# A new order of the first batches, and h as 384 and 192 columns with g stored by units of 192 tokens

## The chip, the cores and the metric

The kernel runs on one NeuronCore of a Trainium2 chip. The metric is the device time of one execution in microseconds. TensorE (PE) multiplies into PSUM; its weight loads have a row of their own in the profile (PEld). VectorE is DVE, ScalarE is ACT, GpSimd is POOL, and SyncE (SP) issues all transfers.

## The reference

```python
# 8 batches, 8 heads, 576 tokens, 64 per head, 32 memory slots
a = exp(phi - max over tokens);  a = a / (sum over tokens + 1e-9)
k_m, v_m = a^T @ k, a^T @ v                       # per head: 32 x 64
attn = softmax((q @ k_m^T) / 8);  y = attn @ v_m
x = y as 4608 x 512
x = relu(x @ w_in1)**2 @ w_out1                   # 512 -> 2048 -> 512
out = silu(x @ w_in2) @ w_out2                    # 512 -> 2048 -> 512
```

All arrays are float32; the four weights come as 64-bit words, of which the kernel makes float32.

## The kernel before

The program has four stages, one after the other: attention fused with the first product (the "first stage", up to about 318 us), the second product with squares taken of g (L889), the third product (L1003), and the fourth (L889 again). The last three use a scheme of seven products for eight and run in blocks of 384 tokens (TH).

**First stage.** For each batch of 576 tokens the value part of the attention is folded into the first weights: `piece` (L546) multiplies the small `v_m` into 512 columns of `w_in1`, and ACT and DVE cut the result into a high and a low float32r half (`wp`). The softmaxed scores, turned, are the moving operand, again as high and low half (`attnT`). `first_product` (L649) makes one tile h per 128 of the 2048 columns: 112 such tiles for batches 1 to 7, numbered by t, each of twelve matmuls, six (two row groups times high-high, high-low, low-high) for each half of the tokens, and a half is 288 columns. h lies in two PSUM banks, one half in each, and there are two h buffers. One ReLU on ACT (L671) writes a row of g into `gt`, and after each second row `to_rows` (L616) sends the pair to the DRAM array `g1`, where 1.5 blocks of 384 tokens make a batch: two transfers, of 384 and of 192 tokens, with a run of 1536 or 768 bytes for each row of the pair on each partition.

Batch 0 goes another way (`first_by_halves`, L626): four tiles t share a group of 512 columns, each with two columns of 128 and one span of the tokens, 256 or 320 of them (`SPANS0`), so that work begins before all tokens have their scores. Its scores are made by token (`scores_by_token`, L502) and turned on PE (`turn_attn`, L530). Weights of batch 0 are loaded in units (`load_unit`, L264; `unit`, L278, makes float32 of one on ACT and DVE).

**Order.** Things are put into a table `sched` by `at(time, function)`, and the table is emptied in order of time between the tiles t: entries below 0 come before the first tile. `START` (L50), the list `tail` in `front` (L310), `UNITS0`, `PIECES0` (L52), `PLAN`, `PLAN1` and `PLAN2` (L54 to L62) hold the times. The tile framework then sets the final order on each engine by its own plan; `follow` adds only an order, `after` and `hold` add a real wait. `in_order` chains the loads of the start. `pe` chains the matmuls before the first tile, and `idle` (L300) puts in matmuls of no use that keep PE busy there. `join` (L451) sets where the first matmul of a front's group comes on PE.

**Buffers that matter.** `kv` has one buffer, so the loads of batch 2's kv have to wait for the product of batch 1; `h` has two, `gt` four.

Of the kernel before, what the change touches and what calls it, by code (L numbers as in the profile page):

```python
# [21 lines left out]
P = 128  # L22
# [4 lines left out]
HALF = S // 2  # L27
NF = DFF // P
NC = 5
# [5 lines left out]
TB, TH = 6, 384  # L35
NQ = NF // 2
# [8 lines left out]
CHUNKS0 = ((0, P), (2 * P, 3 * P, S - P))  # L45
SPANS0 = ((0, 2 * P), (2 * P, S))


IDLE = {2: 7, 3: 6, 4: 7}
START = ("phi", "kv", "idle15", "max", "rows", "idle3", "exp", "idle18", "product", "q", "q", "w0", "w1", "q", *(f"w{n}" for n in range(2, 8)))  # L50
UNITS0 = (6, 6, 7, 7, 9, 9, 10, 10)
PIECES0 = {0: (1, 0), 1: (1, 1), 7: (2, 0), 8: (2, 1), 10: (3, 0), 12: (3, 1)}  # L52
# [25 lines left out]
def attention_moe_moe(ctx: ExitStack, tc, q, kv, phi, w_in1, w_out1, w_in2, w_out2, out):  # L78
# [231 lines left out]
    def front(b):  # L310
# [7 lines left out]
        def load_phi():  # L318
# [3 lines left out]
            held(nc.sync.dma_start(t[:, :NC - 1], phi[b, :n].rearrange("(p c e) -> p c e", p=P, e=2 * P)))  # L322
            held(nc.sync.dma_start(t[:rows(NC - 1), NC - 1], phi[b, n:].rearrange("(p e) -> p e", e=2 * P)))

        def load_kv(c):
# [7 lines left out]
            (hold if b > 1 else in_order)(nc.sync.dma_start(t.rearrange("p k e d -> p (k e d)"), kv[b, c * P:c * P + n]))  # L333
# [11 lines left out]
        def load_q(r):  # L345
            if b == 0:
                if r == 0:
                    st["q"] = apool.tile([P, NP, S], F32, tag="at", name="q")
# [3 lines left out]
            (hold if begun else in_order)(nc.sync.dma_start(t, q[b, r]))  # L352
# [45 lines left out]
        def kv_product(*gs):  # L398
# [4 lines left out]
            for c, g in ((c, g) for c in range(NC) for g in gs):  # L403
                n = rows(c)
                for p in range(NP):
# [5 lines left out]
                    join(mm, c == g == p == 0, new=True)  # L411
# [58 lines left out]
        def scores(r):  # L470
# [12 lines left out]
            nc.scalar.activation(e, e, AF.Exp, scale=1.0 / float(D) ** 0.5)  # L483
# [8 lines left out]
        def transpose_attn(r):  # L492
# [6 lines left out]
            nc.scalar.copy(hi, x)  # L499
            nc.vector.tensor_tensor(lo, x, hi.bitcast(F32), op=ALU.subtract)  # L500

        def scores_by_token(r):  # L502

            cs = CHUNKS0[r]
            n = len(cs)
            ps = bank("pssc").rearrange("p a n -> p (a n)")[:, :n * 2 * P]
            for i, c in enumerate(cs):
                for p in range(NP):
                    to = i * 2 * P + p * 2 * M
                    pe(nc.tensor.matmul(  # L510
                        ps[:, to:to + 2 * M], st["q"][:, p, c:c + P], st["km"][:, p].rearrange("p g m -> p (g m)"),
# [9 lines left out]
            nc.vector.reduce_max(mx[:, :, :, 0], pv, axis=AX.X)  # L521
# [5 lines left out]
            nc.vector.tensor_tensor(ev, ev, sm.to_broadcast([P, 2 * nb, M]), op=ALU.mult)  # L527
            st["e", r] = e.rearrange("p (g t) -> p g t", g=2)

        def turn_attn(r):  # L530
# [15 lines left out]
        def piece(j, h=None):  # L546
# [10 lines left out]
            by_heads(ps[:, :, :PC], 1, lambda p: win[:, 2 * j + h, p], made[2 * j + h])  # L557
# [4 lines left out]
        if b == 0:  # L562
            third = iter(range(NR))
            do = {
                "phi": load_phi, "kv": lambda: [load_kv(c) for c in range(NC - 1)], "max": max_phi, "rows": max_rows,
                "exp": exp_phi, "product": lambda: kv_product(0, 1), "q": lambda: load_q(next(third)),
# [8 lines left out]
            for w in range(8, 2 * NPC):  # L575
# [3 lines left out]
                lambda: scores_by_token(0), lambda: scores_by_token(1), lambda: (unit(0, 0), unit(0, 1)),  # L579
                lambda: idle(6), lambda: piece(0, 0), lambda: idle(9), lambda: turn_attn(0), lambda: idle(5),  # L580
# [514 lines left out]
```

## Time and profile before

| | us |
|---|---|
| median of 3 runs (lowest, highest) | 1381.91 (1380.5, 1383.04) |
| the profiled execution | 1379.26 |
| its span, first to last instruction | 1377.4 |

| engine | busy us | share of the span |
|---|---|---|
| PE | 1356.8 | 99% |
| PE weight loads | 1311.7 | 95% |
| DVE | 982.6 | 71% |
| ACT | 796.1 | 58% |
| POOL | 21.5 | 2% |

The busy time of PE is a union of matmuls that overlap in the pipeline, so a group's busy time says little of what one matmul costs. The cost of one in a run without a stop is the length of the run, less the duration of its last one, divided by the number of steps between the starts. "Idle before" is the time that the engine sat before an instruction, and the arrow names what ended it.

### The profile page before, as it was taken

To read this page: it belongs to the slowest core of one execution; us is meant where nothing else is said; L and a number is where in the kernel's file an instruction comes from. 1 tells how busy PE (TensorE), PEld (TensorE's weight loads), DVE (VectorE), ACT (ScalarE), POOL (GpSimd) and SP (SyncE) were. 2 spreads that over 40 slices of the span, in tenths; PEclk is the share of its full clock that TensorE was granted. 3 is DMA by queue.
4 is the path that set the end of the run, shared out by engine and by line. 5 is a ranking of instruction groups with operands and counts; after the bars stand their busy time and mean duration, and the time that the engine had idled before them with its cause. 6 is when DMAs were issued, how large, how long until landed. Compare 5 with 4: busy or idle time off the path is not lost.

```text
span 1377.4 us, 25465 instructions
## 1 busy us (share of the span) xinstructions
PE 1356.8 (99%) x9349; PEld 1311.7 (95%) x9349; DVE 982.6 (71%) x1602; ACT 796.1 (58%) x1305; POOL 21.5 (2%) x44
## 2 busy tenths in 40 slices
PE   8899999999999999999999999999999999999998
PEld 6778888898999999999999999999999999999998
DVE  4768787747797988989565756566449868768583
ACT  3656666667778686777354645555444444444442
POOL 0000000000000000000000000000000000000000
PEclk9999999999999999999999999999999999999999
DMA  9979999899877978899998787888999567574651
GB/s 325 373 248 339 360 362 328 294 346 356 307 256 274 310 256 299 262 310 340 301 322 299 250 308 269 281 287 285 366 399 355 165 217 244 171 238 159 223 157 35
DMA packets 208446, 388.26 MB, mean 282 GB/s; under 512 B 19264, under 2 KB 90944, under 8 KB 208320
## 3 DMA queue, kind: packets, MB, share of 16 engines
q1 hardware_dynamic: 208320, 386.62, 81.2%
q8 instruction: 74, 1.21, 0.4%
q14 instruction: 52, 0.43, 0.1%
HBM read 253.38 MB, written 133.17 MB: 281 GB/s over the span
## 4 chain that ended last, share of the span: by engine, by line
PE 88%; DMA 9%; SPq 1%; ACT 1%; DVE 1%; issue 0%; ACTq 0%; DVEq 0%
PE psa L889 22%; PE psb L889 15%; PE psa L1003 15%; PE psc L889 15%; PE h L661 9%; PE psc L1003 7%; PE psb L1003 4%; DMA st<-moe_w_in 2%; DMA a<-phi 2%; DMA g<-gt 1%; DMA w1o<-pp 1%; PE pswp L463 1%; PE pskv L407 1%; DMA q<-q 1%; DMA r<-g 1%; DMA kv<-kv 1%
## 5 line engine op out<-in xcount | busy, mean ns | idle before, releaser
L856 DVE TENSOR_TENSOR c<-r,c 128x768 fp32r<-128x768 f32 x336 | 316.5, 955 | 141.4 <-ACT c L855 140.5
L855 ACT CAST c<-r 128x768 fp32r<-128x768 f32 x336 | 279.7, 837 | 233.9 <-PE psa L889 86.1
L889 PE MATMUL psa<-c,ws 128*128 128x384 f32 x1728 | 310.7, 336 | 1.8 <-ACT c L855 1.5
L889 PEld LDWEIGHTS psa<-c,ws 128*128 128x128 f32 x1728 | 301.8, 188 | 2.4 <-ACT c L855 1.7
L1003 PE MATMUL psa<-xc,ws 128*128 128x384 f32 x1152 | 217.9, 336 | 0.0
L889 PE MATMUL psc<-c,ws 128*128 128x384 f32 x1152 | 207.9, 335 | 0.0
L661 PEld LDWEIGHTS h<-at,wp 128*128 128x128 f32 x1344 | 180.1, 188 | 28.7 <-ACT gt L671 16.7
L889 PE MATMUL psb<-c,ws 128*128 128x384 f32 x1152 | 206.3, 336 | 0.0
L1003 PEld LDWEIGHTS psa<-xc,ws 128*128 128x128 f32 x1152 | 202.3, 188 | 0.0
L889 PEld LDWEIGHTS psc<-c,ws 128*128 128x128 f32 x1152 | 201.3, 188 | 0.0
L889 PEld LDWEIGHTS psb<-c,ws 128*128 128x128 f32 x1152 | 201.2, 188 | 0.0
L661 PE MATMUL h<-at,wp 128*128 128x288 f32 x1344 | 190.9, 299 | 4.4 <-ACT gt L671 4.2
L1003 PE MATMUL psc<-xc,ws 128*128 128x384 f32 x576 | 110.8, 335 | 0.0
L1003 PEld LDWEIGHTS psc<-xc,ws 128*128 128x128 f32 x576 | 101.1, 188 | 0.0
L671 ACT ACTIVATE gt<-h 128x576 f32<-128x576 f32 x112 | 72.2, 648 | 35.7 <-PE h L661 25.9
L205 DVE TENSOR_TENSOR pp<-pw,pp 128x256 f32<-128x256 f32 x148 | 63.1, 436 | 32.7 <-ACT pp L204 30.4
L833 ACT ACTIVATE r<-r 128x768 f32<-128x768 f32 x96 | 80.7, 843 | 4.2 <-PE psc L889 3.4
L162 ACT CAST top<-st 128x256 f16<-128x256 bf16 (+1 forms) x112 | 57.9, 526 | 30.5 <-PE psa L1003 12.9
L204 ACT CAST pp<-pw 128x256 fp32r<-128x256 f32 x148 | 58.0, 402 | 29.5 <-PE psa L1003 15.4
L1017 ACT ACTIVATE g2t<-g2t 128x1152 f32<-128x1152 f32 x48 | 54.7, 1164 | 28.1 <-DVE g2t L733 28.1
L166 DVE SCALAR_TENSOR_TENSOR pw<-st,top 128x256 int32<-128x256 int32 x96 | 41.2, 435 | 28.6 <-ACT top L162 28.0
L1003 PE MATMUL psb<-xc,ws 128*128 128x384 f32 x288 | 56.9, 336 | 0.0
(103 smaller groups left out, 1164.3 us busy)
## 6 DMA issues: line engine op xcount, KB each, us to landing
r<-g SPq DMA_DIRECT2D x192, 384.0 KB, 5.8
g<-g2t SPq DMA_DIRECT2D x48, 768.0 KB, 7.0
ws<-w2i SPq DMA_DIRECT2D x136, 256.0 KB, 5.1
ws<-w2o SPq DMA_DIRECT2D x136, 256.0 KB, 4.4
ws<-w1o SPq DMA_DIRECT2D x116, 256.0 KB, 4.5
g<-gt SPq DMA_DIRECT2D x64, 384.0 KB, 5.9
kv<-kv SPq DMA_DIRECT2D x32, 516.0 KB, 6.2
st<-moe_w_out SPq DMA_DIRECT2D x64, 256.0 KB, 5.5
```

The lines of the kernel that those rows point to most:

```text
L162: ins = nc.scalar.copy(top.bitcast(F16).rearrange("p (n h) -> p n h", h=2)[:, :, 1], flat.bitcast(BF16).rearrange("p (n h) -> p n h", h=4) ...
L166: to_f32.last = nc.vector.scalar_tensor_tensor(f.bitcast(I32), flat.rearrange("p (n w) -> p n w", w=2)[:, :n, 1], 13, top, op0=ALU.logical ...
L204: held(nc.scalar.copy(hi, w[:, of]))
L205: tt(lo, w[:, of], hi.bitcast(F32), op=ALU.subtract)
L661: mm = nc.tensor.matmul(h[:, half, :HALF], wp[b, j][:, g, s, fo:fo + P], attnT[b][:, x, g, tk], start=(k == 0), stop=(k == len(ops) - 1),)
L671: relus.append(nc.scalar.activation(gt[:, f % 2].rearrange("p (h t) -> p h t", h=2), h[:, :, :HALF], AF.Relu))
L833: ins = nc.scalar.activation(x, x, AF.Square)
L855: nc.scalar.copy(c[:, 0], r(name))
L856: tt(c[:, 1], r(name), c[:, 0].bitcast(F32), op=ALU.subtract)
L889: mm = nc.tensor.matmul(ps[o][bank], W[h * QS + u][:, slot(n), wi, o * P:(o + 1) * P], x[:, xi, u], start=(first and h == u == m == 0), st ...
L1003: mm = nc.tensor.matmul(ps[q][bank], W[q][:, slot(n), wi, k * P:(k + 1) * P], x[:, xi, k], start=(n in FIRST and k == 0 and m == 0), stop= ...
L1017: nc.scalar.activation(gq[q][:, :3], gq[q][:, :3], AF.Silu)
```

## The change

Four things change. First, **h** of batches 1 to 7 is cut as 384 and 192 columns instead of twice 288: it begins 128 columns into the first bank, so that 384 fill the bank and 192 lie in the next, and the 576 are one stretch. The spans of batch 0 become 192 and 384 tokens instead of 256 and 320. Second, **g**: `gt` and the rows in `g1` are laid out by units of 192 tokens, and within a unit both rows of a pair stand one behind the other, so that a transfer has one run of 3072 or 1536 bytes on each partition. The second stage reads its moving operand as two stretches of 192. Third, **batch 0**: q is loaded in two parts (192 and 384 tokens) whose rows are contiguous, the second behind w0 and w1; the softmax of the first span comes wholly ahead of that of the second on DVE; piece (0,1), the second units and the turn of the second span are put between the first tiles; there are fewer idle matmuls. Fourth, **batches 1 to 7**: kv of batch 2 and phi of batch 3 are loaded behind batch 1's last q; the product, the turn and the times of batch 1 move; from batch 2 on the exponentials of the scores are emitted one tile later and follow the last ReLU in order, the turned scores come one tile later and follow it too.

```diff
+HB = 512 - TH
-CHUNKS0 = ((0, P), (2 * P, 3 * P, S - P))
-SPANS0 = ((0, 2 * P), (2 * P, S))
-IDLE = {2: 7, 3: 6, 4: 7}
-START = ("phi", "kv", "idle15", "max", "rows", "idle3", "exp", "idle18", "product", "q", "q", "w0", "w1", "q", ...)
+CHUNKS0 = ((0, RT - P), (RT, RT + P, S - P))
+SPANS0 = ((0, RT), (RT, S))
+IDLE = {2: 6, 3: 5, 4: 7}
+START = ("phi", "kv", "idle15", "max", "rows", "idle3", "exp", "idle18", "product", "q", "w0", "w1", "q", ...)
-PIECES0 = {0: (1, 0), 1: (1, 1), 7: (2, 0), 8: (2, 1), 10: (3, 0), 12: (3, 1)}
+PIECES0 = {1.2: (1, 0), 1.3: (1, 1), 6.5: (2, 0), 8: (2, 1), 10: (3, 0), 12: (3, 1)}
 PLAN = {
-    "q": (-5, -3, 5), "scores": (4, 8, 12), "attn": (6, 10, 14), "pieces": (4, 8, 12, 16),
+    "q": (-5, -3, 5), "scores": (4, 8, 12), "attn": (7, 11, 15), "pieces": (4, 8, 12, 16),
 PLAN1 = {
-    "phi": -9, "ones": 4, "kv": (-8, -8, -8, -8), "softmax": (1, 2, 3), "product": 5, "turn": 7,
-    "q": (-6.5, 4, 9), "scores": (8, 10, 11), "attn": (10, 11, 13), "pieces": (9, 12, 13, 15),
+    "phi": -9, "ones": 4, "kv": (-8, -8, -8, -8), "softmax": (1.15, 2, 3), "product": 6.6, "turn": 7.5,
+    "q": (-6.5, 4, 8.5), "scores": (8, 10, 11), "attn": (10, 11, 13), "pieces": (9, 12, 13, 15),
-PLAN2 = {**PLAN, "phi": -10, "ones": -5.5, "kv": (-12, -11, -10, -9), "softmax": (-5, -4, -3)}
+PLAN2 = {**PLAN, "phi": -10, "ones": -2, "kv": (-7.4, -7.2, -7, -6.8), "softmax": (-5, -4, -3)}
     def unit(j, i):
-        if begun:
+        if j > 3:
             hold(ins)
         else:
-            after(ins, ready[(i, 1, 2, 4)[j]])
+            after(ins, ready[(0, 1, 2, 4)[j]])
+            if j == 1:
+                follow(to_f32.last, ready[3])
         def load_phi():
+            if b == 3:
+                follow(ins, group["q"])
         def load_kv(c):
+            if b == 2:
+                follow(ins, group["q"])
         def load_q(r):
             if b == 0:
-                in_order(nc.sync.dma_start(st["q"][:, :, r * RT:(r + 1) * RT], q[b, r]))
+                first, end = SPANS0[r]
+                n = P * NP
+                in_order(nc.sync.dma_start(
+                    st["q"][:, NP * first:NP * end], q[b, n * first:n * end].rearrange("(p n) -> p n", p=P),
+                ))
...
+            if b == 1 and r == NR - 1:
+                group["q"] = ins
-        def join(mm, first, new=False):
+        def join(mm, first, new=False, second=False):
-            if first and b > 1:
+            if first and (b > 1 or new and b == 0 and begun):
                 follow(mm, group["h"] if new else group["last"])
+            elif first and b == 1 and second:
+                follow(mm, group["last"])
         def scores(r):
+            st["e", r] = e, ev, sm, nb
+        def softmax(r):
+            e, ev, sm, nb = st["e", r]
+            ins = nc.scalar.activation(e, e, AF.Exp, scale=1.0 / float(D) ** 0.5)
+            if b > 1:
+                follow(ins, relus[-1])
         def transpose_attn(r):
-            nc.scalar.copy(hi, x)
+            ins = nc.scalar.copy(hi, x)
+            if b > 1:
+                follow(ins, relus[-1])
         def scores_by_token(r):
-            nc.vector.reduce_max(mx[:, :, :, 0], pv, axis=AX.X)
+            ins = nc.vector.reduce_max(mx[:, :, :, 0], pv, axis=AX.X)
+            if r:
+                follow(ins, st["mult"])
         def turn_attn(r):
+                    elif i == g == 0:
+                        follow(mm, group["h"])
             tail = (
                 lambda: (kv_scale(0), kv_scale(1)), kv_turn, lambda: idle(7),
-                lambda: scores_by_token(0), lambda: scores_by_token(1), lambda: (unit(0, 0), unit(0, 1)),
-                lambda: idle(6), lambda: piece(0, 0), lambda: idle(9), lambda: turn_attn(0), lambda: idle(5),
-                lambda: (unit(1, 0), unit(1, 1)), lambda: piece(0, 1),
-                lambda: turn_attn(1), lambda: (unit(2, 0), unit(2, 1)), lambda: (unit(3, 0), unit(3, 1)),
+                lambda: scores_by_token(0), lambda: (unit(0, 0), unit(0, 1)), lambda: idle(6), lambda: piece(0, 0),
+                lambda: scores_by_token(1), lambda: idle(3), lambda: turn_attn(0), lambda: idle(5),
             )
+            for n, fn in enumerate((
+                lambda: (unit(1, 0), unit(1, 1)), lambda: piece(0, 1), lambda: (unit(2, 0), unit(2, 1)),
+            )):
+                at(0.1 + n / 10, fn)
+            at(1.1, lambda: (turn_attn(1), unit(3, 0), unit(3, 1)))
+            at(begin + plan["scores"][r] + (1 if b > 1 else 0), lambda r=r: softmax(r))
     def to_rows(b, f, gt):
-        i = 0
-        while i < S:
-            to, k = divmod(b * S + i, TH)
-            n = min(TH - k, S - i)
-            nc.sync.dma_start(g1[to // 2][:, 2 * fh + to % 2, u:u + 2, k:k + n], gt[:, :, i:i + n])
-            i += n
+        j = 0
+        while j < NR:
+            to, half = divmod(b * NR + j, 2)
+            n = min(2 - half, NR - j)
+            rows = g1[to // 2][:, 2 * fh + to % 2, u:u + 2].rearrange("p u n -> p (u n)")
+            nc.sync.dma_start(
+                rows[:, half * 2 * RT:(half + n) * 2 * RT], gt[:, j:j + n].rearrange("p j u n -> p (j u n)"),
+            )
+            j += n
     def first_product(t):
-        h = psum.tile([P, 2, 512], F32, tag="h", bufs=2, name="h")
+        h = psum.tile([P, 2, 512], F32, tag="h", bufs=2, name="h").rearrange("p a n -> p (a n)")[:, HB:HB + S]
-        for half in range(2):
-            tk = slice(half * HALF, (half + 1) * HALF)
+        for tk in (slice(0, TH), slice(TH, S)):
-                    h[:, half, :HALF], wp[b, j][:, g, s, fo:fo + P], attnT[b][:, x, g, tk],
+                    h[:, tk], wp[b, j][:, g, s, fo:fo + P], attnT[b][:, x, g, tk],
-            gts[b] = gpool.tile([P, 2, S], F32, tag="gt", name="gt")
+            gts[b] = gpool.tile([P, NR, 2, RT], F32, tag="gt", name="gt")
-        relus.append(nc.scalar.activation(gt[:, f % 2].rearrange("p (h t) -> p h t", h=2), h[:, :, :HALF], AF.Relu))
+        relus.append(nc.scalar.activation(gt[:, :, f % 2], h.rearrange("p (j n) -> p j n", n=RT), AF.Relu))
     # second(), the second stage alone
+            if square:
+                x = x.rearrange("p i u n -> p i (u n)").rearrange("p i (j u n) -> p i u j n", j=2, n=RT)
-                            ps[o][bank], W[h * QS + u][:, slot(n), wi, o * P:(o + 1) * P], x[:, xi, u],
+                            ps[o][bank].rearrange("p (j n) -> p j n", n=RT) if square else ps[o][bank],
+                            W[h * QS + u][:, slot(n), wi, o * P:(o + 1) * P], x[:, xi, u],
```

## Rows read from the trace of the kernel before

**Rows 1.** busy time by stretch; columns: us, PE, PEld, DVE, ACT, POOL, clock, DMA share, GB/s

```profile
20.00:36.00 16.00, 12.44 (x128) 9.29 (x127) 12.69 (x23) 9.33 (x15) 0.00 (x0) 1.00 1.04 370
...
160.00:290.00 130.00, 130.00 (x1444) 112.99 (x1443) 103.84 (x236) 89.17 (x172) 10.36 (x15) 1.00 0.95 332
290.00:320.00 30.00, 27.18 (x199) 26.15 (x198) 4.72 (x10) 20.69 (x33) 0.00 (x0) 1.00 1.02 365
320.00:662.00 342.00, 342.00 (x1963) 342.00 (x1964) 302.68 (x429) 252.41 (x390) 0.00 (x0) 1.00 0.86 293
```

**Rows 2.** waits of PE; columns: who waited, for whom, us, times, longest

```profile
PE h L661 <- ACT gt L671: 4.2, 6, 1.1
...
PE h L637 <- ACT wp L559: 1.7, 2, 1.2
PE pssc L463 <- DMA q<-q: 1.5, 1, 1.5
PE psa L889 <- ACT c L855: 1.5, 1, 1.5
PE psat L538 <- DVE e L527: 1.1, 1, 1.1
PE pswp L463 <- DVE ssm L525: 1.1, 1, 1.1
```

**Rows 3.** timeline of PE, windows inside three runs; columns: start, length, what, count

```profile
62.16 1.44 PE L637 MATMUL h<-at,wp 128*128 128x256 f32 x10
...
170.91 6.11 PE L661 MATMUL h<-at,wp 128*128 128x288 f32 x44
...
329.70 5.55 PE L889 MATMUL psb<-c,ws 128*128 128x384 f32 x31
```

**Rows 4.** groups by form; columns: what, count, busy us, mean ns of one, idle before

```profile
L889 PE MATMUL psb<-c,ws 128*128 128x384 f32 x1152 | 206.3, 336 | 0.0
...
L661 PE MATMUL h<-at,wp 128*128 128x288 f32 x1344 | 190.9, 299 | 4.4 <-ACT gt L671 4.2
...
L637 PE MATMUL h<-at,wp 128*128 128x256 f32 x96 | 14.5, 292 | 1.9 <-ACT wp L559 1.7 <-DVE at L544 0.3
...
L463 PE MATMUL pswp<-win,kvm 64*32 64x512 f32 x448 | 30.8, 593 | 0.5 <-DVE e L479 0.5
...
L463 PE MATMUL pswp<-win,kvm 64*32 64x256 f32 x128 | 5.4, 385 | 1.1 <-DVE ssm L525 1.1
```

**Rows 5.** timeline of weight loads: one, two after a stop; a run of L510's

```profile
79.44 0.19 PEld L661 LDWEIGHTS h<-at,wp 128*128 128x128 f32 x1 [0.84 <-ACT gt L671]
...
79.44 0.30 PEld L661 LDWEIGHTS h<-at,wp 128*128 128x128 f32 x2 [0.84 <-ACT gt L671]
...
17.77 2.76 PEld L510 LDWEIGHTS pssc<-km,q 128*128 128x128 f32 x24
```

**Rows 6.** timeline of all engines, 13 to 37 us: DVE between the two softmaxes

```profile
22.89 0.96 DVE L521 TENSOR_REDUCE smx<-pssc 128x24 f32<-128x768 f32 x1
...
24.36 0.17 DVE L525 TENSOR_SCALAR ssm<-ssm 128x16 f32<-128x16 f32 x1
```

**Rows 7.** timeline of SP: loads of kv and q around 55 us

```profile
53.03 3.46 SPq L333 DMA_DIRECT2D kv<-kv  x5
...
57.41 0.33 SPq L352 DMA_DIRECT2D q<-q  x1
```

**Rows 8.** timeline of ACT around 98 us: an exponential and a ReLU

```profile
98.08 0.53 ACT L483 ACTIVATE e<-e 128x384 f32<-128x384 f32 x1 [0.28 <-DVE e L482]
98.51 0.63 ACT L671 ACTIVATE gt<-h 128x576 f32<-128x576 f32 x1
```

**Rows 9.** the chain that ended last, at the end of the first stage

```profile
306.50 6.79 DMA g<-gt
```

**Rows 10.** timeline around 153 us: batch 3's last scores and first matmul

```profile
152.93 0.56 DVE L500 TENSOR_TENSOR at<-et,at 128x384 fp32r<-128x384 f32 x1
...
153.09 1.33 PE L661 MATMUL h<-at,wp 128*128 128x288 f32 x8
```

More of the change, by code (lines that the diff above doesn't have):

```diff
@@ L26 @@
 NP = H // 2
-HALF = S // 2
 NF = DFF // P
@@ L321, in load_phi @@
             held = hold if b > 1 else in_order
-            held(nc.sync.dma_start(t[:, :NC - 1], phi[b, :n].rearrange("(p c e) -> p c e", p=P, e=2 * P)))
+            ins = nc.sync.dma_start(t[:, :NC - 1], phi[b, :n].rearrange("(p c e) -> p c e", p=P, e=2 * P))
+            held(ins)
+            if b == 3:
+                follow(ins, group["q"])
             held(nc.sync.dma_start(t[:rows(NC - 1), NC - 1], phi[b, n:].rearrange("(p e) -> p e", e=2 * P)))
@@ L332, in load_kv @@
             t = st["kv"][:n, c]
-            (hold if b > 1 else in_order)(nc.sync.dma_start(t.rearrange("p k e d -> p (k e d)"), kv[b, c * P:c * P + n]))
+            ins = nc.sync.dma_start(t.rearrange("p k e d -> p (k e d)"), kv[b, c * P:c * P + n])
+            (hold if b > 1 else in_order)(ins)
+            if b == 2:
+                follow(ins, group["q"])
             if b == 0:
@@ L410, in kv_product @@
                     ))
-                    join(mm, c == g == p == 0, new=True)
+                    join(mm, c == g == p == 0, new=True, second=True)
                 if b == 0 and g and c in IDLE:
@@ L505, in scores_by_token @@
             n = len(cs)
+            first, end = SPANS0[r]
+            qr = st["q"][:, NP * first:NP * end].rearrange("p (k n) -> p k n", k=NP)
             ps = bank("pssc").rearrange("p a n -> p (a n)")[:, :n * 2 * P]
@@ L510, in scores_by_token @@
                     pe(nc.tensor.matmul(
-                        ps[:, to:to + 2 * M], st["q"][:, p, c:c + P], st["km"][:, p].rearrange("p g m -> p (g m)"),
+                        ps[:, to:to + 2 * M], qr[:, p, c - first:c - first + P], st["km"][:, p].rearrange("p g m -> p (g m)"),
                         start=True, stop=True,
@@ L556, in piece @@
                 return
-            by_heads(ps[:, :, :PC], 1, lambda p: win[:, 2 * j + h, p], made[2 * j + h])
+            by_heads(ps[:, :, :PC], 1, lambda p: win[:, 2 * j + h, p], made[2 * j + h], new=(j, h) == (0, 1))
             hi, lo = (wp[b, j][:, :, i, h * PC:(h + 1) * PC] for i in range(2))
@@ L562, in front @@
         if b == 0:
-            third = iter(range(NR))
+            part = iter(range(2))
             do = {
                 "phi": load_phi, "kv": lambda: [load_kv(c) for c in range(NC - 1)], "max": max_phi, "rows": max_rows,
-                "exp": exp_phi, "product": lambda: kv_product(0, 1), "q": lambda: load_q(next(third)),
+                "exp": exp_phi, "product": lambda: kv_product(0, 1), "q": lambda: load_q(next(part)),
             }
@@ L643, in first_by_halves @@
         if half == 0:
-            gts[pair] = gpool.tile([P, 2, S], F32, tag="gt", name="gt")
-        nc.scalar.activation(gts[pair][:, :, tk], h[:, :, :n], AF.Relu)
+            gts[pair] = gpool.tile([P, NR, 2, RT], F32, tag="gt", name="gt")
+        first, end = (i // RT for i in SPANS0[half])
+        nc.scalar.activation(
+            gts[pair][:, first:end].rearrange("p j u n -> p u j n"), h[:, :, :n].rearrange("p u (j n) -> p u j n", n=RT), AF.Relu,
+        )
         if half:
@@ L661, in first_product @@
                 mm = nc.tensor.matmul(
-                    h[:, half, :HALF], wp[b, j][:, g, s, fo:fo + P], attnT[b][:, x, g, tk],
+                    h[:, tk], wp[b, j][:, g, s, fo:fo + P], attnT[b][:, x, g, tk],
                     start=(k == 0), stop=(k == len(ops) - 1),
                 )
-                if half == k == 0:
+                if tk.start == k == 0:
                     begun.append(mm)
@@ L1075 @@
     a["kv"] = np.pad(x, [(0, 0)] * 4 + [(0, 1)]).reshape(B, S, -1)
-    a["q"] = a["q"].transpose(0, 1, 3, 2).reshape(B, NP, P, NR, RT).transpose(0, 3, 2, 1, 4)
+    x = a["q"].transpose(0, 1, 3, 2).reshape(B, NP, P, S).transpose(0, 2, 1, 3)
+    spans = [[(r * RT, r * RT + RT) for r in range(NR)], SPANS0]
+    a["q"] = np.stack([np.concatenate([x[b, :, :, i:j].reshape(-1) for i, j in spans[b == 0]]) for b in range(B)])
     a["phi"] = chunks(a["phi"].transpose(0, 2, 1, 3).reshape(B, S, 2 * P))
```

11 lines of the change are left out of this document (6 added, 5 removed).

## The prediction

> **What bounds the kernel now.** I read the busy times by stretch first, then the waits of PE, then the spacing of its matmuls. From 320 us on PE is busy without a break at a granted clock of 1.00, its 2.4 GHz level, and inside the first stage it is so from 160 to 290 us [rows 1]. So PE sets the end, and whatever the change adds to a matmul is paid in full. What PE loses by waiting lies at both ends of the first stage: it is busy 12.44 of 16 us from 20 to 36 us and 27.18 of 30 from 290 to 320 [rows 1]. The waits say for whom: the ReLU (4.2 us in six places), the halves of a piece (1.7), a load of q (1.5), the first operand of the second stage (1.5), the first softmax of batch 0 (1.1 twice) [rows 2]. That list, 11.1 us, is nearly all that any reordering can give back.
>
> Next, the price of a matmul. In runs without a stop the step from start to start is (length - duration of one) / (count - 1), less 0.10 us for the first step after a stop, where the weights have still to come. For 384 columns (5.55 - 0.336) / 30 = 174 ns; for 288 (6.11 - 0.299 - 0.10) / 43 = 133 ns; for 256 (1.44 - 0.292 - 0.10) / 9 = 116 ns, between 115 and 118 by the rounding [rows 3, 4]. On that line a column costs about 0.43 ns and 10 ns are fixed: these matmuls are bound by their moving columns.
>
> **The split of h.** Each of the 112 tiles had 12 matmuls of 288 columns and gets 6 of 384 and 6 of 192. On the line 192 columns would take 92 ns, and 174 + 92 = 266 = 2 x 133: nothing would change. But each matmul has a weight load of its own, and the six of 192 stand in a row. After a stop, where nothing else holds the loads back, one load is 0.19 us long and two are 0.30, so the second starts 0.11 us behind the first [rows 5]. A long run says the same: 24 loads of L510, whose matmuls have only 64 columns, are (2.76 - 0.19) / 23 = 112 ns apart [rows 5]. Under a stream of 288 or 384 columns such a load is hidden; under 192 it is not. I take 110 ns for a matmul of 192, between 108 and 112, as both rows show 128 x 128 loads of 4-byte weights. A pair then takes 174 + 110 - 266 = 18 ns more. There are 112 x 6 = 672 pairs, and batch 0, whose 256 + 320 columns become 192 + 384, has 16 x 6 = 96: 768 x 18 ns = **+13.8 us**. With 108 and 112 it is +12.3 and +15.4. No row has a float32r matmul under 256 columns, so the outer bounds are wide: the line, 0, and the rival below on the other side.
>
> **The second stage's operand in two stretches.** 2016 matmuls now read 2 x 192 columns with a gap. A piece's 512 columns come in two stretches of 256, batch 0's 256 in one: 593 against 385 ns, 208 ns for 256 columns in two passes, which at 2.4 GHz are 213 [rows 4]. The gap costs nothing there, and I take nothing; as this is another kind of matmul, 1 ns each (2 us) stays as a bound above.
>
> **Batch 0.** From 20 to 36 us DVE works 12.69 of 16 us [rows 1]: it is the bound there. The maximum of the second span (0.96 us) stands on it in the middle of the first span's softmax, ahead of an addition of 0.17 us that the first tile waits for [rows 6]; units and the second subtraction come between too. The change puts the first span wholly ahead and cuts its q load to 192 tokens, and it moves the second units behind the first tile. The total of DVE's work doesn't shrink, and the third tile still needs the second span, so I give back not all of the 3.56 us that PE idles there but **-2.4** (0 to -3.6).
>
> **Piece and product.** The longer wait for a piece's halves (1.2 us [rows 2]) comes because the product of batch 1 runs ahead of piece (2,0); the one goes from 5 to 6.6, the other from 7 to 6.5: **-1.0** (0 to -1.2).
>
> **q behind kv.** SP issues five loads of batch 2's kv from 53.03 us for 3.46 us, and only behind them the q load for which PE waits 1.5 us, followed by 0.5 for the scores [rows 2, 7]. Now q goes first, some 4 us earlier. What is queued behind it on SP is kv of batch 2 and phi of batch 3, whose users come many tiles later. **-2.0** (0 to -2.2).
>
> **ReLUs.** ACT works in order, and an exponential of 0.53 us stands straight ahead of the ReLU that ends one of the waits [rows 8]. Following the ReLU takes such cases away, not those where a copy of a piece (L554) stands ahead. Of the 4.2 us, 0.9 lie at the end of the stage; of the other 3.3 I take **-1.8** (0 to -3.3).
>
> **End of the stage.** The chain passes through a store of g of 6.79 us [rows 9] before a ReLU gets its buffer. 128 stores with half as many runs, spread over a first stage that is some us longer, should land earlier: **-0.9** of the 2.8 us that PE idles there (0 to -2.4). Elsewhere the stores hide behind PE's work, and their shape costs nothing; if that cover were gone, the bound would be the same few us.
>
> **What the new order can cost.** The turned scores come one tile later. Around 153 us the last low half of batch 3 ends at 152.93 + 0.56 = 153.49, and the batch's first matmul is at 153.09 [rows 10]. Only the seventh needs those tokens: 6 x 133 ns later before, 6 x 174 after, so it starts at 154.13. One tile (12 x 133 = 1.6 us) later the half would end at 155.1, and PE would wait 1.0 us. Six boundaries make 0 to 6 us; this was a late one, and slower tiles give ACT and DVE time: **+0.6**. Behind the ReLUs only ACT's own casts are queued.
>
> **Sum.** 13.8 - 2.4 - 1.0 - 2.0 - 1.8 - 0.9 + 0.6 = +6.3 us. The profiled execution took 1379.26 us (1.9 beside its span), so it would take 1385.6; the median of the runs is 2.65 above it, and the forecast is 1381.9 + 6.3 = **1388.2**.
>
> **The rivals.** *The short matmul is not held by its load.* If loads can be pulled further ahead than these rows show, 192 columns take 92 ns, the split costs nothing, and the rest, -7.5 us, stands: 1374.4, faster than before. It decides at 768 pairs: the change breaks even at 102 ns for 192 columns. For it speaks that the straight line holds down to 256; against it that no two full loads lie under 0.1 us apart in the rows, after a stop or in a run [rows 5]. Beside this: the Trainium skill (TensorE: Matmul & The Clock Gate, "Back-to-back issue gap") gives about 81 ns for 128 columns and 131 for 512 in a stream of load and matmul; an estimate on the line between them is 89 ns for 192, by which the split would be free and the time this rival's. The trace doesn't agree for these weights, since 384 columns already take 174 ns.
>
> *Nothing is given back.* The tile framework orders by its own plan, so waits may only move, and the turned scores come late at the boundaries: 13.8 + 3 = +16.8, 1398.7. For it: DVE-bound starts [rows 1] and the thin margin [rows 10]. Against it: the q load, whose place on SP is set by the order alone.
>
> *Short float32r matmuls run at another rate.* Under 256 columns the trace has only plain float32, two instructions of two passes each. A pass rate of half would give 2 x 80 + 10 = 170 ns and 768 x (174 + 170 - 266) = +60 us, 1434. No row speaks for it.
>
> **How the numbers follow.** The forecast's case gets 0.70, the free load 0.15, nothing given back 0.10, the other rate 0.05. Around the forecast the bounds of the parts give 1381 to 1396; the range reaches down to the first rival and up to the second: 1373 to 1398. A measurement of this kernel tells about 0.2%, 2.8 us. The forecast's case is slower by more with 0.75 of its chance, the same with 0.21, faster with 0.04. So faster 0.15 + 0.03 = 0.18, same 0.15, slower 0.52 + 0.10 + 0.05 = 0.67.
>
> **What would show it.** In the profile after, weight loads and matmuls of 192 columns 108 to 112 ns apart say that the split costs what I say; 92 refute it, and the forecast with it. A tile should take 1.70 us instead of 1.60, and the second stage should keep 174 ns. PE should no longer wait for a q load, and less for ReLUs behind an exponential; the first tile of batch 0 should start near 26 us, its third near 34. New waits for L500 at a batch's seventh matmul would show the price of the later turn. A drop of the granted clock between 20 and 36 us, where fewer idle matmuls fill PE, would add to the start.

## The result and the profile after

The changed kernel takes 1389.84 us (median, 1389.21 to 1392.50), the kernel before 1381.91 (1380.07 to 1383.10): ratio 1.0057, interval 1.0046 to 1.0068, so 7.9 us slower, or 6.4 to 9.4. The forecast was 1388.2, within 1373 to 1398. The profiled execution took 1389.84 us, its span is 1388.1.

First the busy time by stretch, with the columns of [rows 1]:

```profile
20.00:36.00 16.00, 13.30 (x127) 9.99 (x127) 12.44 (x22) 7.71 (x14) 0.00 (x0) 0.90 1.04 358
...
160.00:290.00 130.00, 130.00 (x1366) 116.05 (x1365) 99.79 (x224) 85.02 (x165) 9.84 (x14) 1.00 0.90 319
290.00:331.00 41.00, 39.05 (x297) 36.41 (x297) 12.55 (x26) 26.82 (x45) 0.83 (x1) 1.00 0.89 331
...
330.00:662.00 332.00, 331.63 (x1904) 331.24 (x1903) 292.42 (x415) 245.85 (x383) 0.00 (x0) 1.00 0.86 293
```

PE is still busy without a break from 160 to 290 us, but in these 130 us it gets 1366 matmuls done where it was 1444 [rows 1]. The end of the first stage has moved: the second stage begins at 329.65 us instead of 319.00. From 290 us to just behind that point PE lost 2.8 us before [rows 1] and loses 1.95 now. One wait for a ReLU (0.86 us before) is gone; the two waits for the first operands of the second stage (1.5 and 0.4 us) are still there. From 20 to 36 us the granted clock is 0.90 instead of 1.00: a part of that stretch ran at the lower level (more on this below).

The waits of PE, to be laid beside [rows 2]:

```profile
...
PE psa L933 <- ACT c L897: 1.5, 1, 1.5
PE pskv L423 <- POOL kv L343: 1.3, 1, 1.3
PE h L703 <- ACT gt L713: 1.2, 2, 0.7
PE pswp L481 <- DVE mx L392: 0.9, 1, 0.9
PE h L677 <- ACT wp L592: 0.9, 1, 0.9
PE h L677 <- DVE at L577: 0.7, 1, 0.7
PE pst L451 <- ACT y L439: 0.6, 1, 0.6
```

The wait for q (1.5 us) is gone, and that for ReLUs has fallen from 4.2 us in six places to 1.2 in two. The longer wait for a piece's halves (1.2 us, within batch 0) is gone as well; one of 0.9 at the start of batch 0 is there. New is a wait of 0.6 us for `y`, the product that ACT scales before it is turned. Still the kernel is slower, so PE's own work must have grown by more than these waits shrank.

It has. Timeline of PE inside one tile, windows that hold only some of its matmuls, first of 384 and then of 192 columns; columns: start, length, what, count:

```profile
184.61 0.85 PE L703 MATMUL h<-at,wp 128*128 128x384 f32 x4
184.79 0.51 PE L703 MATMUL h<-at,wp 128*128 128x384 f32 x2
...
185.40 0.72 PE L703 MATMUL h<-at,wp 128*128 128x192 f32 x5
185.40 0.61 PE L703 MATMUL h<-at,wp 128*128 128x192 f32 x4
```

and of the weight loads in the same row of short matmuls:

```profile
185.42 0.41 PEld L703 LDWEIGHTS h<-at,wp 128*128 128x128 f32 x3
185.53 0.30 PEld L703 LDWEIGHTS h<-at,wp 128*128 128x128 f32 x2
```

Two matmuls of 384 columns more are 0.34 us, 0.17 a step; one of 192 more is 0.11, and one weight load more is 0.11. So the short matmuls and their weight loads go at one pace. Which of the two sets it this row can't tell, as each matmul has one load; the loads after a stop [rows 5] and the cuts below speak to that. From the starts of single matmuls in all 112 tiles (medians): the first of 384 columns in a tile takes 200 ns, the next five 173 to 175, the first of 192 takes 88, the next five 111 to 114. Together this is 1.72 us a tile, where twelve of 288 columns took 12 x 133 = 1.60.

The second stage, whose operand now lies in two stretches, has not changed; this is the row of the first group of [rows 4] in the changed kernel (half of its matmuls are the second stage's, the others the fourth's, whose operand is as before):

```profile
L933 PE MATMUL psb<-c,ws 128*128 128x384 f32 x1152 | 206.3, 336 | 0.0
```

Where the time goes can be followed from batch to batch. The starts of the first matmul of h in a batch, in us, from the traces (the last two kernels are experiments below):

| start of | before | after | orders alone | 384/192, orders of before |
|---|---|---|---|---|
| batch 0 | 29.14 | 26.80 | 25.88 | 28.68 |
| batch 1 | 74.60 | 76.70 | 72.25 | 74.73 |
| batch 2 | 117.36 | 119.44 | 115.65 | 116.44 |
| batch 3 | 153.09 | 156.13 | 151.56 | 153.33 |
| batch 4 | 188.73 | 192.81 | 187.92 | 190.01 |
| batch 5 | 223.50 | 229.50 | 222.68 | 226.70 |
| batch 6 | 258.47 | 266.19 | 257.92 | 263.56 |
| batch 7 | 290.35 | 299.99 | 289.79 | 297.36 |
| second stage | 319.00 | 329.65 | 319.06 | 327.37 |

Batches 4 and 6 are longer by 1.92 us, the whole price of their tiles (16 x 0.12 us). Batch 1 isn't longer at all, and batches 2, 3 and 7 by 1.0 us each. Batch 0 begins 2.3 us earlier and is 4.4 us longer (49.90 against 45.46). With the orders alone it is 46.37, so 0.9 of this come with them; in a kernel below with the same start and no drop of the clock it is 49.04, so 2.7 come with the spans of 192 and 384, and 0.9 with the drop. From the start of the second stage to the end it is 1058.4 us in both kernels. The profiles differ by 10.7 us and the medians by 7.9, since the profiled execution of before was 2.6 us faster than its median and that of after lay on its own.

### The profile page after: what moved, and what is told of

Read it like the earlier page. It is cut to its first block, busy times and chain, and to the rows that moved or that the text cites. A ratio compares the mean times of both kernels' runs of the same rounds, so it can differ in the third digit from the quotient of the medians.

```text
span 1388.1 us, 25457 instructions
## 1 busy us (share of the span) xinstructions
PE 1372.1 (99%) x9341; PEld 1328.8 (96%) x9341; DVE 985.6 (71%) x1602; ACT 795.5 (57%) x1305; POOL 21.9 (2%) x44
## 4 chain that ended last, share of the span: by engine, by line
PE 93%; DMA 3%; DVE 2%; ACT 1%; SPq 0%; issue 0%; POOL 0%; ACTq 0%; POOLq 0%
PE psa L933 22%; PE psb L933 14%; PE psa L1048 14%; PE psc L933 14%; PE h L703 12%; PE psc L1048 7%; PE psb L1048 4%; PE pswp L481 2%; PE pskv L423 1%; PE h L677 1%; DMA kv<-kv 1%; PE pssc L481 1%; DMA g<-gt 0%; DMA ws<-w1o 0%; DMA r<-g 0%; DMA st<-moe_w_out 0%
## 5 line engine op out<-in xcount | busy, mean ns | idle before, releaser
L703 PEld LDWEIGHTS h<-at,wp 128*128 128x128 f32 x1344 | 196.0, 190 | 23.1 <-ACT gt L713 16.0
L933 PE MATMUL psb<-c,ws 128*128 128x384 f32 x1152 | 206.3, 336 | 0.0
L703 PE MATMUL h<-at,wp 128*128 128x384 f32 (+1 forms) x1344 | 203.5, 308 | 1.4 <-ACT gt L713 1.2
```

Of the source, the lines that this page charges most:

```text
L703: mm = nc.tensor.matmul(h[:, tk], wp[b, j][:, g, s, fo:fo + P], attnT[b][:, x, g, tk], start=(k == 0), stop=(k == len(ops) - 1),)
L933: mm = nc.tensor.matmul(ps[o][bank].rearrange("p (j n) -> p j n", n=RT) if square else ps[o][bank], W[h * QS + u][:, slot(n), wi, o * P:(o ...
```

## The experiments

**Is the short matmul held by its load?** Three other cuts of the 576 columns, each made by the start of h in its bank and the two slices:

```diff
-HB = 512 - TH
+HB = 512 - 288
-        for tk in (slice(0, TH), slice(TH, S)):
+        for tk in (slice(0, 288), slice(288, S)):
```

> The changed kernel with h of batches 1 to 7 again as two times 288 columns, as one stretch over two banks; all else as changed. Theory, the weight load binds the short matmuls: a tile goes from 1.717 us back to 1.60, 112 tiles give 13.5 us, so 1389.8 - 13.5 = 1376.3 (0.996 of the kernel before), and no two matmuls of h are under 125 ns apart. Rival, the split was free and the time went into the new order: 1389.8 stays.

Measured: 1382.04 us, ratio 0.9998 (0.9986 to 1.0009). So the changed kernel loses its 7.8 us with the cut of h alone, but nothing is left over: neither the 1376.3 of the theory nor the 1389.8 of the rival came. The waits for ReLUs are back:

```profile
PE h L703 <- ACT gt L713: 5.0, 7, 1.6
```

> The changed kernel with h as 352 and 224 columns. Theory, load bound: 224 columns stream in 106 ns by the line and are held at 111 by their loads, 352 take 161, a pair 272 against 266: +4 us on the version with 288, 1380.3. Rival, short matmuls run at a slower rate per column (111 ns for 192 less 10 fixed is 0.53 ns each): 224 take 128, a pair 289, +15.5, 1391.8. Rival, columns alone count: 1376.3.

Measured: 1382.92 us, ratio 1.0002 (0.9988 to 1.0016). With 416 and 160 columns:

> The changed kernel with h as 416 and 160 columns. Theory, load bound: 160 columns take no less than 111 ns, as 192 do, and 416 take 189, a pair 300: +34 ns x 672 = 22.8 us on the version with 288, 1399.1. Rival, a slower rate per column: 160 take 95, a pair 284, +12.1, 1388.4. Rival, columns alone count: 1376.3.

Measured: 1396.27 us, ratio 1.0097 (1.0073 to 1.0121). Timelines of PE inside a tile, first of 224 columns, then of 160:

```profile
183.55 0.72 PE L703 MATMUL h<-at,wp 128*128 128x224 f32 x5
183.55 0.61 PE L703 MATMUL h<-at,wp 128*128 128x224 f32 x4
```

```profile
185.54 0.57 PE L703 MATMUL h<-at,wp 128*128 128x160 f32 x4
185.54 0.46 PE L703 MATMUL h<-at,wp 128*128 128x160 f32 x3
```

One matmul more is 0.11 us with 224, 192 and 160 columns alike. That decides for a pace that doesn't depend on the columns, as the load gives it, and against a price by columns, which would have given 1388.4 for the last cut. That cut came out 2.8 us below the expected 1399.1: its pairs take the 300 ns foreseen, but the 23 us that this adds to 112 tiles also swallow the waits for ReLUs, 5.0 us with twice 288 columns and none in the list of this cut, so that the time grows by 14.2 us only. The time with 224 columns, 2.6 us above what was expected, shows the same as that with 288: the waits for ReLUs come back as the tiles get shorter (4.9 us in six places).

**Would another order of the same matmuls hide the load?** The 384 and the 192 columns of one weight matrix stand one behind the other:

```diff
-        for tk in (slice(0, TH), slice(TH, S)):
-            ops = [(g, s, x) for g in range(2) for s, x in ((0, 0), (0, 1), (1, 0))]
-            for k, (g, s, x) in enumerate(ops):
+        ops = [(g, s, x) for g in range(2) for s, x in ((0, 0), (0, 1), (1, 0))]
+        for k, (g, s, x) in enumerate(ops):
+            for tk in (slice(0, TH), slice(TH, S)):
```

> The changed kernel; in each tile of batches 1 to 7 the 384 and the 192 columns of one weight matrix stand one behind the other, instead of six matmuls of 384 and then six of 192. Theory (one load ahead: the load of the next matmul has only the stream of the present one to hide in): 384 stays at 174 ns, 192 stays at 111, a pair 285; a tile 6 x 285 = 1.71 us as before, the time 1389.8 within 0.2%. Rival (loads run further ahead, and only a row of short matmuls uses up the lead): two loads of 107 ns hide in a pair, 174 + 92 = 266 ns, a tile 1.60 us, 112 x 0.12 = 13 us less of PE's work, of which some 5 come back as waits for ReLUs: about 1382.

Measured: 1389.09 us, ratio 1.0060 (1.0044 to 1.0076), no better. A pair takes 287 ns, as expected within 2, but not as expected in its parts: the starts of single matmuls in all 112 tiles give 198 to 199 ns for 384 and 88 for 192, not 174 and 111. These are the 200 and the 88 of the one change between lengths that a tile of the changed kernel has at each end of its rows. So the rival (loads hidden, 266) falls, but the picture of a load that hides only in the matmul just ahead doesn't give these steps either. Why the pair comes to 287 here, where two loads at 0.11 us would fit into 266, stays open. No run lets several matmuls in a row use one set of weights, which would part the load from any other limit of a row of short matmuls.

**The cut alone on the kernel before.**

```diff
-        h = psum.tile([P, 2, 512], F32, tag="h", bufs=2, name="h")
+        h = psum.tile([P, 2, 512], F32, tag="h", bufs=2, name="h").rearrange("p a n -> p (a n)")[:, 512 - TH:512 - TH + S]
-        for half in range(2):
-            tk = slice(half * HALF, (half + 1) * HALF)
+        for tk in (slice(0, TH), slice(TH, S)):
...
```

> The kernel before with one thing changed: h of batches 1 to 7 as 384 and 192 columns (batch 0, the layout of g and all orders stay). Theory: +13.5 us on 1381.9, less up to 3 us of waits for ReLUs that slower tiles hide: 1392.4 to 1395.4. Rival, the split is free: 1381.9.

Measured: 1389.96 us, ratio 1.0049 (1.0034 to 1.0065): 7.7 us over the 1382.31 of the kernel before in that session (6.8 by the ratio), where 112 tiles x 0.12 us make 13.4. This is 2.4 us below the lower end of what was expected. The waits of PE in it say where most of the rest is:

```profile
...
PE pssc L463 <- DMA q<-q: 2.1, 1, 2.1
PE h L637 <- ACT wp L559: 1.7, 2, 1.2
...
PE h L660 <- ACT gt L670: 0.8, 2, 0.6
```

Nothing in the order was changed here, and still the waits for ReLUs go from 4.2 us to 0.8. What made them shrink in the changed kernel was the slower tile, not the new order behind the ReLUs. The table shows it by batch: batches 1, 2, 3 and 7 take up some of the price. The stretch that holds most of batch 1, first in the kernel before and then in this one, with the columns of [rows 1]:

```profile
75.00:118.00 43.00, 40.87 (x498) 33.37 (x497) 29.21 (x69) 25.47 (x49) 2.78 (x4) 1.00 0.86 302
```

```profile
75.00:118.00 43.00, 42.82 (x504) 36.73 (x504) 29.78 (x69) 26.25 (x52) 2.78 (x4) 1.00 0.87 307
```

PE's idle time goes from 2.13 us to 0.18. A stop costs more than its idle time: the matmul ahead of it counts as busy for 299 ns instead of one step of 133 [rows 4], and the first step behind it is 235 to 240 ns in the kernel before. By this estimate each stop that goes gives 0.27 us more, and four stops fewer with 3.4 us of waits make 4.5 of the 5.2 us by which this profile's way from batch 1 to the second stage falls short of 13.4 (table: 252.64 against 244.40 us).

**The orders, one at a time.** q ahead of kv and phi, with the change's times for product, turn and piece (2,0), on the kernel before:

```diff
+            if b == 2:
+                follow(ins, group["q"])
...
-PIECES0 = {0: (1, 0), 1: (1, 1), 7: (2, 0), ...}
+PIECES0 = {0: (1, 0), 1: (1, 1), 6.5: (2, 0), ...}
-    ..., "softmax": (1, 2, 3), "product": 5, "turn": 7,
+    ..., "softmax": (1.15, 2, 3), "product": 6.6, "turn": 7.5,
...
```

> The kernel before with batch 1's last q ahead of batch 2's kv and batch 3's phi on SP, and with the product, turn and piece (2,0) of the change; h as 2 x 288, old layout of g, old order of the softmaxes. The prediction's terms: the wait for q (1.5 us and 0.5 behind it) and the wait for a piece's halves (1.2 us) go, batch 1 begins at 71.6 us instead of 74.6, and the median falls by 3.0, to 1379.3 beside a before of 1382.3. Rival: both waits go, but other waits in batch 0 take their place; batch 1 begins within 1 us of 74.6, no change.

Measured: 1381.24 us, ratio 0.9986 (0.9970 to 1.0001). Batch 1 starts at 73.02 instead of 74.60 (0.4 of this is an earlier first tile, which the edit doesn't touch), between what the theory and the rival said. The wait for q is gone, but the waits for ReLUs grow, and within batch 0 there is a new one for `y`, which ACT scales later now that the product comes later:

```profile
PE h L670 <- ACT gt L680: 6.2, 6, 1.6
...
PE pst L444 <- ACT y L432: 1.0, 1, 1.0
```

Then the exponentials and the turned scores, later and behind the last ReLU, alone on the kernel before:

```diff
-    ..., "attn": (6, 10, 14), ...
+    ..., "attn": (7, 11, 15), ...
+            if b > 1:
+                follow(ins, relus[-1])
...
```

> The kernel before with only the exponentials and turned scores later and behind the ReLUs (from batch 2 on). The prediction's term: -1.8 us, two of the five waits of PE for a ReLU between 95 and 157 us go. Rival, ACT is simply full there beside tiles of 1.60 us: the waits stay between 3 and 6 us in all and the time does not change (within 1 us). Rival, turned scores come late at batch starts: up to +6 us, PE waits for L500.

Measured: 1382.15 us, ratio 1.0004 (0.9992 to 1.0016), the waits for ReLUs 3.6 us in five places. Nothing is won.

Next the changed kernel with the orders of batches 0 and 1 as before, and its columns and layout as they are:

```diff
-                lambda: scores_by_token(0), lambda: (unit(0, 0), unit(0, 1)), lambda: idle(6), lambda: piece(0, 0),
-                lambda: scores_by_token(1), lambda: idle(3), lambda: turn_attn(0), lambda: idle(5),
+                lambda: scores_by_token(0), lambda: scores_by_token(1), lambda: (unit(0, 0), unit(0, 1)),
+                lambda: idle(6), lambda: piece(0, 0), lambda: idle(9), lambda: turn_attn(0), lambda: idle(5),
...
```

> The changed kernel with the orders of batches 0 and 1, of kv, phi and q as before; spans of 192 and 384 tokens, h as 384 and 192, the layout of g and the later scores stay. The prediction's terms: batch 0's new order, piece and q together gave 5.4 us, so 1389.8 + 5.4 = 1395.2. Rival, as the version with 288 columns suggests: the new order of batch 0 gave back what it took, 1388 to 1391.

Measured: 1389.46 us, ratio 1.0054 (1.0034 to 1.0074). With the old order the first tile starts 3.0 us later (29.82 against 26.80), but batch 1 at 76.72 against 76.70. The second number holds a drop of the granted clock, to 0.50 from 32.68 to 36.09 us, that the profile with the old order doesn't have there. In the kernel with alternating columns, whose start is that of the changed one and whose clock stayed at 1.00, batch 1 starts at 74.93. So the new orders are worth up to 1.8 us at this place here; the medians, 1389.46 against 1389.84, show nothing of it.

**All orders, with the columns and the layout of before.** This is the cleanest of them:

```diff
-HB = 512 - TH
+HB = 512 - 288
-CHUNKS0 = ((0, RT - P), (RT, RT + P, S - P))
-SPANS0 = ((0, RT), (RT, S))
+CHUNKS0 = ((0, P), (2 * P, 3 * P, S - P))
+SPANS0 = ((0, 2 * P), (2 * P, S))
...
```

and g's tile and rows as before.

> The changed kernel with every column count and the layout of g as before: h as twice 288 columns, the spans of batch 0 256 and 320 tokens. What is left of the change are its orders alone. The prediction's terms for the orders give 1381.4 - 2.4 - 1.0 - 2.0 - 1.8 + 0.6 = 1374.8. Theory from the runs so far (the orders give about nothing, for ReLUs take back what q and the piece give; the 96 pairs of 384 and 192 columns in batch 0 cost 96 x 20 ns = 1.9 us): 1.9 less than the run with 288 columns and batch 0 as 192 and 384, so 1380. Rival (batch 0 is bound by DVE, so its matmuls' columns cost nothing): 1382.

Measured: 1381.15 us against 1381.18, ratio 1.0002 (0.9993 to 1.0011): the orders as a whole are worth nothing that can be told. The time lies between the theory's 1380 and the rival's 1382 and doesn't decide between them. Batch 1 starts 2.35 us earlier than before (table), the second stage 0.06 later. The waits of PE say what took most of it back:

```profile
PE h L697 <- ACT gt L707: 6.3, 6, 2.2
...
PE psa L925 <- ACT c L891: 2.3, 1, 2.3
...
PE pst L451 <- ACT y L439: 1.0, 1, 1.0
```

Against [rows 2] the ReLUs have grown by 2.1 us and the first operand of the second stage by 0.8; the wait for `y`, within batch 0, is new. The timeline of ACT in batch 1, in which the first products of batch 2's front begin, shows how a ReLU comes late:

```profile
92.55 0.41 ACT L204 CAST pp<-pw 128x256 fp32r<-128x256 f32 x1 [0.49 <-DVE pw L166]
92.86 1.00 ACT L587 CAST wp<-pswp 128x1024 fp32r<-128x1024 f32 x1
93.77 0.48 ACT L162 CAST top<-st 128x256 f16<-128x256 bf16 x1
94.11 0.51 ACT L506 ACTIVATE e<-e 128x384 f32<-128x384 f32 x1
94.53 0.64 ACT L707 ACTIVATE gt<-h 128x576 f32<-128x576 f32 x1
```

For about 2 us ACT works through a cast of a weight, a copy of a piece, another cast and an exponential before the ReLU at 94.53, for which PE waits 2.15 us. The exponential does follow a ReLU, the one before. Behind one ReLU is ahead of the next. Over a longer stretch ACT is far from full (25.47 of 43 us above), so it is the bunching that counts. This is read from the traces; no run takes work off ACT.

**A piece's copy behind the ReLU.** If the copy is moved too, does ACT come free? On the run with q first:

```diff
+        def halves(j):
+            ps = st.pop(("piece", j))
+            hi, lo = (wp[b, j][:, :, i] for i in range(2))
+            ins = nc.scalar.copy(hi, ps)
+            if relus:
+                follow(ins, relus[-1])
+            nc.vector.tensor_tensor(lo, ps, hi.bitcast(F32), op=ALU.subtract)
...
+            at(begin + plan["pieces"][j] + (1 if b > 1 else 0), lambda j=j: halves(j))
```

> The kernel before with q ahead of kv and phi as in the first of the runs on orders, and from batch 2 on the cut of a piece into halves emitted one tile later and following the last ReLU. Theory (a copy of a piece that stands ahead of a ReLU on ACT makes PE wait for the ReLU): the waits for ReLUs fall from 6.2 us to 3 or less, the time is 1379. Rival (ACT is full in batches 1 to 3, so what is moved behind one ReLU stands ahead of the next): waits of 5 to 7 us, 1381 to 1382.

Measured: 1381.47 us, ratio 1.0001 (0.9990 to 1.0011); the waits for ReLUs are 4.6 us in four places, between the two expectations, and the time is the rival's. No kernel of this study is faster than the one before by more than its interval.

**Layout.** The changed kernel with g's tile, rows and operand as before.

```diff
-            gts[b] = gpool.tile([P, NR, 2, RT], F32, tag="gt", name="gt")
+            gts[b] = gpool.tile([P, 2, S], F32, tag="gt", name="gt")
-        relus.append(nc.scalar.activation(gt[:, :, f % 2], h.rearrange("p (j n) -> p j n", n=RT), AF.Relu))
+        relus.append(nc.scalar.activation(gt[:, f % 2], h, AF.Relu))
...
```

> The changed kernel with the tile gt, the rows in g1 and the second stage's operand as before (two transfers of a pair in runs of 1536 or 768 bytes, one stretch of 384 columns as operand). Theory: the layout is worth nothing either way but for the end of the first stage, 1389.8 + 0 to 1 us, and 384 columns of the second stage stay at 174 ns. Rival (stores with short runs hold back the ReLUs and the first operand of the second stage): the end of the first stage is 1 to 2.4 us later, 1391 to 1392.

Measured: 1388.28 us, ratio 1.0049 (1.0031 to 1.0068). The layout gives nothing and costs nothing that can be told; a store of 384 KB lands after 5.7 us (median) with the old rows and 5.6 with the new, and batch 7 with what follows takes 29.53 us against 29.66.

**Idle matmuls against a drop of the clock.** In the run with twice 288 columns, eight idle matmuls fill the stop behind piece (0,1).

```diff
-                lambda: (unit(1, 0), unit(1, 1)), lambda: piece(0, 1), lambda: (unit(2, 0), unit(2, 1)),
+                lambda: (unit(1, 0), unit(1, 1)), lambda: (piece(0, 1), fill(8)), lambda: (unit(2, 0), unit(2, 1)),
...
```

> The changed kernel with h as 2 x 288 and 8 matmuls of no use between piece (0,1) and the second tile of batch 0, where PE waits for the halves of the piece. Theory, PE's short stops there let the granted clock fall to its 1.2 GHz level for 3.4 us, which costs 1 to 1.7 us: clock 1.00 from 27 to 36 us, 1 us less than without them, 1381. Rival: the clock falls elsewhere in the start (as at 24.8 us in the version without them) and nothing is won.

Measured: 1381.64 us, ratio 0.9994 (0.9983 to 1.0006): 0.4 us below the run without them, inside both intervals. In its profile the clock stays at 1.00 from 27 to 36 us and drops from 324.8 to 328.2 us instead. This decides nothing.

## Why the prediction held

The number came out 1.6 us too low, but two of its steps were wrong by far more, in opposite directions: the split costs 7.8 us instead of 13.8, and the orders and the layout give nothing that can be told instead of 7.5. Batch 0's share of the 13.8, 96 pairs, can't be seen in the medians (ratio 0.9998 with spans of 192 and 384, 1.0002 with those of before, both with twice 288 columns). The price of a matmul was foreseen; that the sum came so near is luck.

- **The price of the split: right.** 192 columns at 110 ns were foreseen and 111 measured; a pair was to cost 18 ns more and costs 20; a tile was to take 1.70 us and takes 1.72. Not foreseen is how a pair's time lies at a change of length: the first short matmul takes 88 ns and the first long one 200, so 174 + 110 holds for a whole row and not for each pair. Both loads in the rows of before, two after a stop and 24 in a run [rows 5], gave the right number for matmuls the trace had never shown. The rival of the free load (92 ns, 1374.4) is refuted by three cuts, and with it the estimate of 89 ns beside it from the Trainium skill (TensorE: Matmul & The Clock Gate, "Back-to-back issue gap"); for these weights the rows decide. The rival of another rate (170 ns) is refuted too.
- **"Whatever the change adds to a matmul is paid in full": wrong.** Here the step failed. It was read from two stretches in which PE is busy throughout [rows 1], 160 to 290 and from 320 us on, and carried to all 112 tiles. The same paragraph put PE's waits "at both ends of the first stage", but 3.3 of the 4.2 us for ReLUs lie between 99 and 158 us. In batches 1 to 3 and at the end of batch 7 PE had waited for ReLUs, behind bunched work on ACT. There a longer tile first uses up that wait. So 13.4 us of work cost 7.7 when added to the kernel before, and gave back 7.8 when taken from the changed one. The prediction counted the same 4.2 us of [rows 2] as something that only an order could win.
- **q behind kv (-2.0), piece and product (-1.0): the waits went, the time not.** Both waits vanish as foreseen, and batch 1 starts 1.6 us earlier with these two alone. Still in batch 0 the later product brings a wait of 1.0 us for `y`, and later the waits for ReLUs rise from 4.2 to 6.2 us. Of the 3.0 us, 1.2 are left in the medians (1381.24 against 1382.47), and the interval of the ratio, 0.9970 to 1.0001, hardly excludes nothing.
- **ReLUs (-1.8): wrong.** The order alone gives 0 (1382.15 against 1382.47). The wait's label named the ReLU, and a row showed an exponential ahead of it [rows 8]; but what came late was a bunch of work on ACT, not this one neighbour (read from one timeline).
- **Batch 0 (-2.4): wrong for the most part.** With all orders and the spans of before the first tile starts 3.3 us earlier (25.88 against 29.14), but the third, which needs the second span, only 1.2 earlier (33.78 against 34.94). Batch 1 starts 2.35 us earlier, for batch 0, the piece and q together (foreseen 5.4); q and the piece alone gave 1.6 of that. By batch 4 only 0.8 is left, at the second stage nothing. With spans of 192 and 384 and a clock of 1.00 batch 1 starts at 74.93, 2.7 us behind this and 0.3 behind the kernel before; 96 pairs at 20 ns explain 1.9 of the 2.7.
- **First tile near 26, third near 34: right within the spread of single executions, but for the clock.** They were at 26.80 and 35.69 in the profile after, and at 25.89 and 33.84 in that of the kernel with alternating columns, which starts the same way but ran at a granted clock of 1.00. The drop of the clock between 20 and 36 us that the prediction named as a possible cost did come in the profile after, and batch 0 is 0.9 us longer with it.
- **End of the stage (-0.9), later turn (+0.6): both nothing.** The layout alone changes neither the landing of the stores nor the end. No wait of PE for turned scores appears in batches 1 to 7. Of the 2.8 us at the end, the 0.86 us for a ReLU are gone in the profile after, as slower tiles fill them; the waits for the first operands of the second stage are as long as before.
- **The second stage's operand (0, up to +2): 0**, by the equal rows.

So the sum was +13.8 - 7.5 = +6.3, and the chip gave +7.8 and 0. "Nothing is given back" was put at 1398.7 and 0.10: that waits only move was true, but turned scores never came late, and its price, the split in full, was wrong too. The forecast's mechanism for the split held, and half of that rival's for the orders. Waits for ReLUs explain the first miss and most of the second: they shrink when PE's work grows, and grow when time is won ahead of them.

## What to carry to other kernels

Price work that is added to the bounding engine by the stretches in which it waits for nothing; where it waits for a second engine, added work can vanish in that wait, and time won ahead of it can come back as more of it. Before reordering for a wait, read what the named engine did in the 2 us ahead: if it was busy throughout, moving one item behind the current tile puts it ahead of the next. And a row of short matmuls, each with weights of its own, costs a weight load each: with these weights cut 288 and 288, not 384 and 192.

## What the runs showed of the hardware

- Float32r matmuls of 160, 192 and 224 columns with 128 x 128 weights of their own each take 110 to 115 ns in a row (the weight loads of such a row start 0.11 us apart too). Only the first of a row, behind a long one, goes at 75, 88 and 102 ns (160, 192, 224); the first long one behind such a row takes 228, 200 and 170 ns (416, 384, 352). Above that the step is 133 (288), 160 (352), 174 (384) and 187 ns (416).
- A moving operand in two stretches of 192 columns costs as much as one of 384: 336 ns each, 206.3 us for 1152 in both, of which the second stage's half has two stretches in the changed kernel.
- The granted clock falls from the 2.4 GHz to the 1.2 GHz level for 3.4 us at a time. The fourteen profiles hold eleven such drops, in two places. Five begin between 24.8 and 32.7 us, all in the eight kernels with the new order of batch 0; the six with the old order have none there. Six begin 0.8 to 2.0 us behind the first matmul of the second stage, ahead of which PE had waited for 1.5 us or more; the other eight profiles have that wait and no drop. Over whole executions the clock is 0.996 to 1.000 in the kernel before and 0.997 to 0.999 in the changed one, so the new order needn't cost clock in sum. Timeline of PE in the changed kernel, between 33 and 36 us:

```profile
33.24 1.48 PE L569 MATMUL psat<-ident,e 128*128 128x128 f32 x6
34.65 1.11 PE L481 MATMUL pswp<-win,kvm 64*32 64x256 f32 x16
```

and the same work in the kernel with alternating columns, at a granted clock of 1.00:

```profile
32.08 0.88 PE L569 MATMUL psat<-ident,e 128*128 128x128 f32 x6
32.88 0.66 PE L481 MATMUL pswp<-win,kvm 64*32 64x256 f32 x16
```

PE had stopped for 0.85 and 0.55 us ahead of this in the one, for 0.85 and 0.56 in the other, so these stops alone don't decide it. Batch 0 was 49.90 us long with the drop and 49.04 without. In the run with 288 columns the drop of the start came earlier, from 24.78 us, while PE was busy throughout (5.00 of 5 us, granted clock 0.66 on average); its last stop ahead, of 0.58 us, had ended at 22.11:

```profile
24.00:29.00 5.00, 5.00 (x31) 4.39 (x31) 4.84 (x10) 2.59 (x5) 0.00 (x0) 0.66 1.03 381
```

What brings it on was not found.
